# Load order, dummy matmuls, one PSUM drain and the weight folds in the first stage of a fused linear-attention and MLP kernel

## The chip, the cores and the metric

The kernel runs on one core of one Trainium2 chip. The metric is the device time of one execution in microseconds. Every execution also lists its span (first to last instruction) and the mean clock that TensorE was granted; the time is about 2.1 us more than the span (183.99 and 181.9). The engines are PE (TensorE matmul), PEld (TensorE weight load), DVE (VectorE), ACT (ScalarE), POOL (GpSimd) and SP (SyncE, which here only issues DMAs). PSUM is the name of the memory of the banks that the matmuls here write (`bank<-wv,xnT` in the profile) and that ScalarE or DVE then reads out (`xnT<-bank`, 0.60 us for 128x512; "drains").

## The reference, cut to what matters

With `x` of 2048 tokens by 448, two branches read the same normalised input:

```python
xn  = layernorm(x)                                  # (2048, 448)
# branch A: linear attention, 16 heads of 28
q, k, v = split(xn @ wqkv)
phi(t)  = concat(softmax(t @ w_phi), softmax(-(t @ w_phi)))    # per head
o   = phi(q) @ (phi(k).T @ v) / (phi(q) @ sum(phi(k)) + 1e-6)
A   = o @ wo
# branch B: token-shift mixer and MLP
h   = gelu(layernorm(xn) @ w1)
x1  = xn + shifted(h) @ w2
B   = x1 + gelu(layernorm(x1) @ w3) @ w4
out = x + A + B
```

The kernel multiplies `w_phi` into the K and Q columns of `wqkv` on the chip ("folds": `wpk`, `wpq`), so that K and Q need one matmul each. Tokens are worked in 16 tiles of 128.

## The kernel before: the parts that the change touches

Every operation is recorded and later emitted on its engine in program order. Semaphore waits are derived from what each operation reads and writes. All matmuls are recorded by one helper line, L203, transposes by L207, ScalarE's activations by L211, other elementwise work by L215, and DMA transposes by L218; so the profile's lines are told apart by their operands.

The loads. SP and ACT issue to a DMA queue each (on the page of before q1 with 12.64 MB and q10 with 1.92 MB, which is what ACT's issues add up to; cuts marked `...`):

```python
        load_x(0, 1)                 # SP
        load_x(1, 1, "ACT")
        load_x(2, 1)                 # SP
        load_x(3, 1, "ACT")
        load_lap(wv, A_wqkv[:, 896:1344], ("ACT", "SP"))   # two halves of wv
        load_x(4, 2)
        load_x(6, 2)
        load_wT(1); load_wT(0)       # 8 DMA transposes of K's and Q's weights, on SP
        ...
        load_lap(w1, B_w1, ("ACT", "ACT"))
        load_x(8, 4, "ACT")
        load_x(12, 4, "ACT")
        R.dma(wphi[0:CR, :, :], ..., "ACT")
```

The normalisation of the 16 tiles is a sequence on DVE and POOL. The statistics of tile `i` stand on DVE ahead of the scaling of tile `i-1`:

```python
        for i in range(10):
            ln1_stats(i, 1, 0)                 # DVE: bn_stats, bn_aggr; POOL: rs
            if i not in (0, 4):
                ln1_apply(dve, i - 1)          # DVE: xn of tile i-1
            if i == 3:
                ln1_apply(dve, 3)
        ...
        for i in range(12, NT):
            xn_Td(i)                           # DMA transposes of tiles 12 to 15, on SP
```

The first matmul stage. There are four pairs of PSUM banks, 0 to 3. `xn_T(i, b)` transposes tile `i` on TensorE into pair `b`, and ScalarE copies it to `xnT`. `V(i, k)` is half `k` of the V projection of tiles `i, i+1`; `v_out(i, b)` drains it (ScalarE). `W(g, m, k)` is half `k` of W1's column pair `m` for token group `g`; `w1_out` is its gelu (ScalarE). `FO(1, ..)` folds K's weights, `FO(0, ..)` Q's; their second half is followed by DVE's casts to `wpk` or `wpq`. `spin` issues dummy matmuls that nothing reads.

```python
        vps = {i: v_pair(i, b) for i, b in ((0, 2), (2, 3), (4, 2), (6, 3), (8, 3), (10, 2))}
        wps = {(g, m): w1_pair(g, m, b) for g, m, b in (..., (3, 0, 0), (3, 2, 2))}
        fps = {(t, m): fold_pair(t, m, b) for t, m, b in ((1, 0, 2), (1, 2, 3), (0, 0, 1), (0, 2, 3))}

        spin(19, 256)
        play([(xn_T, 0, 0), (spin, 3, 256), (xn_T, 1, 1), (spin, 2, 256), V(0, 0), (xn_T, 2, 0), V(0, 1), (xn_T, 3, 1),
              ...
              (w1_out, 0, 2, 1), V(4, 0), V(6, 0), V(4, 1), (v_out, 4, 2), V(6, 1), W(1, 0, 0), (xn_T, 8, 2),
              (v_out, 6, 3), W(1, 2, 0), (xn_T, 9, 2), W(1, 0, 1), (xn_T, 10, 2), W(1, 2, 1), (xn_T, 11, 2),
              (w1_out, 1, 0, 0), (w1_out, 1, 2, 1), V(8, 0), V(10, 0), V(8, 1), (v_out, 8, 3), V(10, 1),
              ...
              FO(1, 2, 0), W(2, 2, 1), (w1_out, 2, 2, 1), FO(1, 2, 1), W(3, 0, 0), W(3, 2, 0), FO(0, 0, 0),
              W(3, 0, 1), (w1_out, 3, 0, 0), FO(0, 0, 1), FO(0, 2, 0), W(3, 2, 1), (w1_out, 3, 2, 2), FO(0, 2, 1)])
```

The loop that follows starts with K's pair (banks of pair 1), then W2's pair (pair 2), and goes on with Q.

The softmax here doesn't subtract the row's maximum and nothing guards it: scores larger than these inputs give would overflow.

## Time and profile before

| | before |
|---|---|
| timed executions | 182.07, 182.23, 182.28 us |
| the profiled execution | 183.99 us, span 181.9, clock 0.991 |
| TensorE busy | 174.4 us, 96% of the span |
| granted clock 0.50 | from 7.93 to 11.35 us |

Part 2 of the page of before cuts the span into 40 slices. Each digit is the busy share of TensorE, or the granted clock, in tenths:

```profile
PE   7699999999999999999999999999999999999993
PEclk9879999999999999999999999999999999999999
```

The clock dips in the second and third slices, 4.5 to 13.6 us, and nowhere else in this row. The table by windows of before, cut at the clock's own steps, shows what came ahead of the dip. The columns are the window, its length, then busy time of PE, PEld, DVE, ACT and POOL with the count of instructions, then the granted clock, the DMA share and GB/s:

```profile
4.52:7.93 3.41, 1.91 (x27) 0.97 (x25) 2.73 (x9) 0.93 (x2) 2.55 (x7) 1.00 1.02 330
7.93:11.35 3.42, 3.42 (x31) 2.14 (x32) 2.62 (x7) 0.76 (x2) 1.66 (x5) 0.50 1.43 336
11.35:14.76 3.41, 3.33 (x39) 2.31 (x39) 3.31 (x10) 2.13 (x4) 2.46 (x7) 1.00 0.91 126
```

In a window of 3.41 us TensorE was busy for 1.91 us, and the next 3.41 us ran at half clock. These are lines of the timeline of before; each has its start, its length, the operation with its shapes, and in brackets the idle time ahead of it with what ended that:

```profile
7.91 1.91 PE L203 MATMUL bank<-wv,xnT 64*128 64x448 bf16 x8 [0.77 <-DMA wv<-in_A_wqkv_dram]
...
23.22 0.29 PE L207 MATMUL bank<-ident,xn 64*128 64x64 bf16 x8 [0.34 <-POOL wpq L215]
...
24.40 2.93 PE L203 MATMUL bank<-wv,xnT 64*128 64x448 bf16 x28
27.18 1.89 PE L203 MATMUL bank<-xnT,w 64*112 64x512 bf16 x16
...
31.00 1.93 PE L203 MATMUL bank<-xnT,w 64*112 64x512 bf16 x16
...
35.28 0.93 PE L203 MATMUL bank<-wpk,xnT 64*128 64x448 bf16 x7 [0.23 <-DVE wpq L215]
35.86 1.10 PE L203 MATMUL bank<-w,hT 64*128 64x448 bf16 x8
```

In order: the first V pair waits for `wv`; the transposes of tile 10 wait; the V pair of tile 8 starts at 24.40; W1's second last group (tiles 8 to 11) at 27.18, its last (tiles 12 to 15) at 31.00; K's first pair waits for the casts of `wpq`; W2's first pair starts at 35.86 with no wait of its own.

### The profile page before, as it was taken

What the parts mean: (1) busy time and instruction counts of PE and PEld (TensorE: products, weight loads), DVE (VectorE), ACT (ScalarE), POOL (GpSimd) and SP (SyncE); (2) the same over time, 40 slices, a digit from 0 to 9 for tenths busy, and PEclk for the clock granted to TensorE, in tenths of its full rate; (3) what the DMA queues carried; (4) which work ended last, traced back from release to release, by engine and by line L of the source; (5) the groups of instructions that cost most, each with busy time, mean ns of one, the idle gap of its engine ahead of it and who ended that gap; (6) DMA issues with size and microseconds to landing.
All of it is one profiled execution on the core that took longest, in us unless ns stands there. A gap on an engine that the chain in (4) does not pass through costs nothing.

```text
span 181.9 us, 5076 instructions
## 1 busy us (share of the span) xinstructions
PE 174.4 (96%) x2196; PEld 100.3 (55%) x2196; DVE 112.5 (62%) x282; ACT 82.5 (45%) x92; POOL 96.0 (53%) x140
## 2 busy tenths in 40 slices
PE   7699999999999999999999999999999999999993
PEld 5357546645587976566445454554555545545451
DVE  5799816669799699835465984641545517465521
ACT  2247875579778887744822422422224213224000
POOL 4666850007779989990065939562350622622740
PEclk9879999999999999999999999999999999999999
DMA  5993277990001110113011341323323120311331
GB/s 125 343 227 71 51 91 212 395 364 15 0 4 29 32 29 4 41 34 73 4 29 32 60 89 30 83 66 71 64 55 83 38 74 0 83 29 29 83 85 45
DMA packets 32981, 14.87 MB, mean 82 GB/s; under 512 B 24704, under 2 KB 32448, under 8 KB 32960
## 3 DMA queue, kind: packets, MB, share of 16 engines
q1 hardware_dynamic: 30192, 12.64, 28.7%
q10 hardware_dynamic: 2768, 1.92, 3.3%
q8 instruction: 17, 0.28, 0.7%
q14 instruction: 4, 0.03, 0.1%
HBM read 7.08 MB, written 1.84 MB: 49 GB/s over the span
## 4 chain that ended last, share of the span: by engine, by line
PE 74%; DVE 10%; POOL 6%; DMA 5%; issue 1%; SPq 1%; ACT 1%; DVEq 0%
PE bank L203 74%; DMA xtok<-in_A_x_dram 4%; DVE xn L215 3%; DVE st L215 3%; POOL rs L215 2%; POOL phik L215 2%; DVE ksum L215 2%; DMA gT<-g_tok 1%; DVE mv L215 1%; POOL xn L215 1%; DVE wpq L215 1%; SPq L221 1%; POOL mv L215 1%; DVE rks L215 1%; ACT phik L211 1%
## 5 line engine op out<-in xcount | busy, mean ns | idle before, releaser
L211 ACT ACTIVATE phik<-bank 128x1024 bf16<-128x1024 f32 (+1 forms) x44 | 42.4, 986 | 62.1 <-PE bank L203 62.1
L203 PE MATMUL bank<-gT,w 64*128 64x512 bf16 x392 | 50.5, 377 | 0.6 <-DMA gT<-g_tok 0.3
L215 DVE TENSOR_TENSOR vaug<-bank,vaug 128x464 f32<-128x464 f32 (+3 forms) x65 | 32.6, 512 | 23.9 <-PE bank L203 22.3
L203 PE MATMUL bank<-w,phik 64*128 64x448 bf16 (+1 forms) x420 | 45.0, 349 | 0.1
L215 POOL TENSOR_TENSOR xnT<-vaug 128x196 bf16<-128x196 f32 (+1 forms) x32 | 18.1, 588 | 47.6 <-DVE vaug L215 47.6
L203 PEld LDWEIGHTS bank<-w,phik 64*128 64x128 bf16 (+1 forms) x420 | 21.7, 94 | 21.7 <-PE bank L203 0.5
L215 POOL TENSOR_TENSOR phik<-phik,rks 128x896 bf16<-128x896 bf16 x16 | 26.8, 1699 | 10.5 <-DVE rks L215 10.5
L203 PEld LDWEIGHTS bank<-gT,w 64*128 64x128 bf16 x392 | 18.4, 94 | 18.4 <-ACT phik L211 1.6
L215 POOL TENSOR_TENSOR vaug<-xn,xtok 128x448 f32<-128x448 bf16 x16 | 16.2, 1034 | 1.2 <-DVE vaug L215 1.2
L215 DVE TENSOR_REDUCE ksum<-phik 128x32 f32<-128x896 bf16 x16 | 16.8, 1048 | 0.0
L203 PE MATMUL bank<-w,hT 64*128 64x448 bf16 (+1 forms) x128 | 16.4, 349 | 0.2 <-DVE xn L215 0.2
L203 PE MATMUL bank<-wv,xnT 64*128 64x448 bf16 x112 | 15.2, 378 | 1.1 <-DMA wv<-in_A_wqkv_dram 0.8
L215 DVE TENSOR_TENSOR xn<-bank,xn 128x256 bf16<-128x256 f32 (+1 forms) x32 | 10.2, 381 | 9.7 <-PE bank L203 9.7
L203 PE MATMUL bank<-xnT,wpq 64*128 64x512 bf16 x112 | 16.1, 376 | 0.0
L203 PE MATMUL bank<-wpk,xnT 64*128 64x448 bf16 x112 | 15.4, 349 | 0.2 <-DVE wpq L215 0.2
L215 DVE RECIPROCAL vaug<-bank 128x16 f32<-128x16 f32 x16 | 4.1, 257 | 17.9 <-PE bank L203 17.9
L203 PE MATMUL bank<-xnT,w 64*112 64x512 bf16 x112 | 15.0, 381 | 0.0
L203 PE MATMUL bank<-wo,xnT 64*128 64x448 bf16 (+1 forms) x106 | 13.4, 349 | 0.0
L215 POOL TENSOR_TENSOR rs<-mv,mhalf 128x1 f32<-128x1 f32 (+2 forms) x17 | 11.7, 690 | 1.4
L215 POOL TENSOR_SCALAR g_tok<-xn,rs 128x512 bf16<-128x512 bf16 x16 | 12.2, 773 | 0.2
L211 ACT ACTIVATE xnT<-bank 128x512 bf16<-128x512 bf16 x12 | 7.1, 597 | 9.6 <-PE bank L207 9.6
L203 PEld LDWEIGHTS bank<-w,hT 48*128 48x128 bf16 (+1 forms) x128 | 8.6, 94 | 4.8 <-DVE xn L215 1.2
(63 smaller groups left out, 181.2 us busy)
## 6 DMA issues: line engine op xcount, KB each, us to landing
w<-in_B_w_dram SPq DMA_DIRECT2D x2, 896.0 KB, 6.6
out_dram<-vaug SPq DMA_DIRECT2D x15, 112.0 KB, 1.9
w<-in_B_w_dram SPq DMA_DIRECT2D x1, 1568.0 KB, 11.9
xtok<-in_A_x_dram ACTq DMA_DIRECT2D x2, 448.0 KB, 8.4
xtok<-in_A_x_dram SPq DMA_DIRECT2D x2, 224.0 KB, 7.0
w<-in_B_w_dram ACTq DMA_DIRECT2D x2, 224.0 KB, 7.1
wo<-in_A_wo_dram SPq DMA_DIRECT2D x2, 224.0 KB, 8.3
w<-in_B_w_dram SPq DMA_DIRECT2D x1, 392.0 KB, 3.7
```

The costliest lines, as they stand in the source:

```text
L203: self.op("PE", lambda e: e.matmul(out, lhsT, rhs, start=start, stop=stop, skip_group_check=True), [out], [lhsT, rhs], tile=self._tile(lhsT))
L211: self.op("ACT", lambda e: e.activation(out, in_, func, **kw), [out], [in_] + aps)
L215: self.op(eng, lambda e: getattr(e, name)(out, *args, **kw), [out], aps)
L221: self.op(eng, lambda e: e.dma_start(out, in_), [out], [in_], dma=True)
```

## The change

It has three parts, which I call A, B and C from here on. A: the first half of `wv` is loaded ahead of `x3`, and four dummy matmuls instead of two bridge the time to the first V pair; the aim is that V starts sooner (the wait for `wv` was 0.77 us) and that the clock does not fall to 0.50. B: the V drain of tile 6 moves behind the transposes of tiles 9 and 10, which should not wait for ScalarE (0.34 us). C: the Q folds are done sooner, so that K's first pair does not wait for DVE's casts (0.23 us).

```diff
-        load_x(3, 1, "ACT")
-        load_lap(wv, A_wqkv[:, 896:1344], ("ACT", "SP"))
+        load_lap(wv, A_wqkv[:, 896:1344], ("ACT", "SP"))
+        load_x(3, 1, "ACT")
...
-        play([..., (xn_T, 1, 1), (spin, 2, 256), V(0, 0), ...
+        play([..., (xn_T, 1, 1), (spin, 4, 256), V(0, 0), ...
...
-              (v_out, 6, 3), W(1, 2, 0), (xn_T, 9, 2), W(1, 0, 1), (xn_T, 10, 2), W(1, 2, 1), (xn_T, 11, 2),
+              W(1, 2, 0), (xn_T, 9, 2), W(1, 0, 1), (xn_T, 10, 2), (v_out, 6, 3), W(1, 2, 1), (xn_T, 11, 2),
...
-              ..., W(3, 0, 0), W(3, 2, 0), FO(0, 0, 0),
-              W(3, 0, 1), (w1_out, 3, 0, 0), FO(0, 0, 1), FO(0, 2, 0), W(3, 2, 1), (w1_out, 3, 2, 2), FO(0, 2, 1)])
+              ..., W(3, 0, 0), FO(0, 0, 0), W(3, 2, 0),
+              FO(0, 0, 1), FO(0, 2, 0), W(3, 0, 1), (w1_out, 3, 0, 0), W(3, 2, 1), (w1_out, 3, 2, 2), FO(0, 2, 1)])
```

More of the change, by code (lines that the diff above doesn't have):

```diff
@@ L752, in bass_parallel_sum__linear_kernel_hedgehog__mixer_s_mlp__prompt_kernel @@
         spin(19, 256)
-        play([(xn_T, 0, 0), (spin, 3, 256), (xn_T, 1, 1), (spin, 2, 256), V(0, 0), (xn_T, 2, 0), V(0, 1), (xn_T, 3, 1),
+        play([(xn_T, 0, 0), (spin, 3, 256), (xn_T, 1, 1), (spin, 4, 256), V(0, 0), (xn_T, 2, 0), V(0, 1), (xn_T, 3, 1),
               (spin, 2, 256), V(2, 0), (v_out, 0, 2), W(0, 0, 0), (xn_T, 4, 2), V(2, 1), (v_out, 2, 3),
@@ L756, in bass_parallel_sum__linear_kernel_hedgehog__mixer_s_mlp__prompt_kernel @@
               (w1_out, 0, 2, 1), V(4, 0), V(6, 0), V(4, 1), (v_out, 4, 2), V(6, 1), W(1, 0, 0), (xn_T, 8, 2),
-              (v_out, 6, 3), W(1, 2, 0), (xn_T, 9, 2), W(1, 0, 1), (xn_T, 10, 2), W(1, 2, 1), (xn_T, 11, 2),
+              W(1, 2, 0), (xn_T, 9, 2), W(1, 0, 1), (xn_T, 10, 2), (v_out, 6, 3), W(1, 2, 1), (xn_T, 11, 2),
               (w1_out, 1, 0, 0), (w1_out, 1, 2, 1), V(8, 0), V(10, 0), V(8, 1), (v_out, 8, 3), V(10, 1),
               (v_out, 10, 2, "DVE"), W(2, 0, 0), W(2, 2, 0), FO(1, 0, 0), W(2, 0, 1), (w1_out, 2, 0, 0), FO(1, 0, 1),
-              FO(1, 2, 0), W(2, 2, 1), (w1_out, 2, 2, 1), FO(1, 2, 1), W(3, 0, 0), W(3, 2, 0), FO(0, 0, 0),
-              W(3, 0, 1), (w1_out, 3, 0, 0), FO(0, 0, 1), FO(0, 2, 0), W(3, 2, 1), (w1_out, 3, 2, 2), FO(0, 2, 1)])
+              FO(1, 2, 0), W(2, 2, 1), (w1_out, 2, 2, 1), FO(1, 2, 1), W(3, 0, 0), FO(0, 0, 0), W(3, 2, 0),
+              FO(0, 0, 1), FO(0, 2, 0), W(3, 0, 1), (w1_out, 3, 0, 0), W(3, 2, 1), (w1_out, 3, 2, 2), FO(0, 2, 1)])
         def w2_norm(i):
```

## The prediction

> **What bounds it now.** TensorE is busy 96% of the 181.9 us span (page, part 1), and 74% of the chain that ended last is matmuls (part 4). From 35.3 us on it waits only about 1 us in all (list of waits), so only the first 35 us can give anything, and a saving there should reach the end.
>
> Four losses lie there (timeline of TensorE, table by windows):
> - The granted clock is 0.50 from 7.93 to 11.35 us, one stretch of 3.41 us. [...] In the window before it, 4.52 to 7.93, TensorE was busy only 1.9 us. The first V pair then takes 1.91 us for 8 matmuls, later ones about 0.8. Up to 1.7 us is lost.
> - 0.77 us idle until wv lands (7.58 and 7.78 us; first matmul 7.91).
> - 0.34 us idle at 23.2 us before the transposes of tile 10. The waits name POOL; I believe it is ScalarE's copy of tile 9 (to 23.07), which ran behind tile 6's V drain (21.67 to 22.58).
> - 0.23 us idle at 35.28, K's first pair waiting for VectorE's wpq casts (from 33.94).
>
> Normalised tiles are not the limit: tile 10 is ready at 19.6 and transposed at 23.2; the room is about 2 us.
>
> **The change, costed.**
> 1. wv's first half ahead of x3: lands perhaps 2 us sooner, x3 that much later (its statistics start at 6.39, so nearly free). But ScalarE issues DMAs until 6.96 and copies tile 1 only from 7.50 to 8.09, which the pair's second matmul needs. So the pair starts 0.25 us sooner and gains about 0.1.
> 2. Two more dummies: about 0.2 us more activity, inside idle time. With the pair's sooner start, the window rises from 1.9 to about 2.4 us busy of 3.41. Whether that keeps the clock this trace doesn't show; I give it 55%. If kept: V0 ends near 9.0 and tile 4's transposes come at 12.4 instead of 13.5; about 1.2 us gained.
> 3. V drain of tile 6 moved: tile 10's transposes about 0.2 sooner, but the drain now ends near 24.75, and the V pair of tile 8, which writes the same banks, must wait for it: 24.8 instead of 24.4. Net loss about 0.3.
> 4. Q folds sooner: K's wait (up to 0.5) goes. But gelu of the last W1 group is later: its second drain ends near 36.05 instead of 35.78, and the W2 pair needs those banks. Net between 0.3 gained and 0.3 lost.
>
> **Sum.** Clock kept: about 181.3. Clock lost: about 182.5. I say 181.8 us, range 180.8 to 182.9. Faster by over 2%: 0.02; within 2%: 0.97; slower: 0.01.
>
> **What would show it.** Step 1: wv landing before 7 us, first V matmul near 7.65, the second still near 8.1. Step 2: no 0.50 clock between 7.9 and 11.4, 8 V matmuls in about 0.9 us. Step 3: no idle at tile 10, a new wait of TensorE for ScalarE's V drain before tile 8's V pair. Step 4: no wait for wpq, a wait for ScalarE's gelu before the first W2 pair.
>
> **What would make it wrong.** [...] a late x3 holding up VectorE's statistics by more than the 2 us of room.

Two passages on what sets the clock are cut out of it, and marked: a sentence on the stretch of half clock, and two clauses of the last paragraph, the second of which said that the times might split by about 1.2 us. The trace did not show what they said of the clock. No term of the sum is cut: 55% of 181.3 and 45% of 182.5 make the 181.8 us.

## The result, and the profile after

The changed kernel took 182.89, 183.22, 182.91 and 182.61 us (median 182.9); before took 182.07 to 182.28 in four executions (median 182.19). The ratio is 1.004, 95% interval 1.0022 to 1.0058. Ratios in this document are the mean time of one kernel's runs over that of the other's runs of the same rounds, so they are not quite the ratios of the medians that are quoted. All four executions of the changed kernel show a clock of 0.998 to 1.00, and the profiled one has a span of 180.8 us: 1.1 us less than the profiled one of before, although the timed executions are 0.7 us slower. The two profiles are thus not of the same kind.

The first two windows of the table of the changed kernel, cut at the same times as before (its own first clock step is at 5.23 us, and 5.23 to 8.64 us has TensorE busy for 2.89):

```profile
4.52:7.93 3.41, 2.89 (x33) 1.51 (x33) 2.87 (x9) 1.19 (x2) 2.32 (x6) 1.00 1.01 327
7.93:11.35 3.42, 3.34 (x44) 1.88 (x42) 2.42 (x8) 2.00 (x3) 1.80 (x6) 1.00 1.20 301
```

TensorE's lines in the timeline of the changed kernel that answer to those of before:

```profile
7.43 1.15 PE L203 MATMUL bank<-wv,xnT 64*128 64x448 bf16 x8
...
21.09 0.29 PE L207 MATMUL bank<-ident,xn 64*128 64x64 bf16 x8
...
22.88 2.82 PE L203 MATMUL bank<-wv,xnT 64*128 64x448 bf16 x28 [0.43 <-ACT vaug L211]
25.54 1.89 PE L203 MATMUL bank<-xnT,w 64*112 64x512 bf16 x16
...
29.78 1.07 PE L203 MATMUL bank<-xnT,w 64*112 64x512 bf16 x8 [0.42 <-ACT hT L211]
...
33.45 0.92 PE L203 MATMUL bank<-wpk,xnT 64*128 64x448 bf16 x7
34.85 0.93 PE L203 MATMUL bank<-w,hT 64*128 64x448 bf16 x8 [0.48 <-ACT hT L211]
```

Each wait that the change aimed at is gone: `wv`, tile 10, the casts. Three others have come: 0.43 us for the moved V drain (`vaug`) ahead of tile 8's V pair, 0.42 us ahead of W1's last group, and 0.48 us for the gelu ahead of W2's first pair. One line of DVE's timeline of the changed kernel is new as well, the statistics of `x3`:

```profile
6.80 0.63 DVE L215 BATCH_NORM_STATS2 st<-xtok 128x6 f32<-128x448 bf16 x1 [0.19 <-DMA xtok<-in_A_x_dram]
```

To say where 0.7 us came from, I first needed an ordinary execution of before to compare with.

### The profile page after: what moved, and what is told of

Same layout as the page of the kernel before. It is cut to its first block, busy times and chain, and to the rows that moved or that the text cites. A ratio compares the mean times of both kernels' runs of the same rounds, so it can differ in the third digit from the quotient of the medians.

```text
span 180.8 us, 5080 instructions
## 1 busy us (share of the span) xinstructions
PE 173.3 (96%) x2198; PEld 100.1 (55%) x2198; DVE 112.6 (62%) x282; ACT 82.7 (46%) x92; POOL 95.7 (53%) x140
## 4 chain that ended last, share of the span: by engine, by line
PE 74%; DVE 10%; POOL 6%; DMA 4%; ACT 2%; issue 2%; ACTq 0%; DVEq 0%
PE bank L203 74%; DVE xn L215 3%; DVE st L215 3%; DMA xtok<-in_A_x_dram 3%; POOL rs L215 2%; POOL phik L215 2%; DVE ksum L215 2%; DMA gT<-g_tok 1%; DVE mv L215 1%; ACT hT L211 1%; POOL mv L215 1%; DVE rks L215 1%; ACT phik L211 1%; ACTq L221 0%; ACT vaug L211 0%
## 5 line engine op out<-in xcount | busy, mean ns | idle before, releaser
L203 PE MATMUL bank<-wpk,xnT 64*128 64x448 bf16 x112 | 14.7, 349 | 0.0
L203 PE MATMUL bank<-wv,xnT 64*128 64x448 bf16 x112 | 13.6, 351 | 0.7 <-ACT vaug L211 0.4
L203 PEld LDWEIGHTS bank<-w,hT 64*128 64x128 bf16 (+1 forms) x128 | 8.4, 94 | 5.7 <-DVE xn L215 1.2
```

Of the source, the lines that this page charges most:

```text
L203: self.op("PE", lambda e: e.matmul(out, lhsT, rhs, start=start, stop=stop, skip_group_check=True), [out], [lhsT, rhs], tile=self._tile(lhsT))
```

## The experiments

Sixteen kernels ran, four to a chip, each beside 11 executions of before on the same chip. All gave correct results. Means are over the executions at full clock (0.998 to 1.00), and the difference is to the mean of the executions of before beside them.

| run | edit on before | executions us | clock 0.991 | mean | difference |
|---|---|---|---|---|---|
| e0_before_again | none | 181.91 to 182.00 | 0 of 5 | 181.95 | -0.23 |
| a_only | A | 181.99 to 182.54 | 0 of 5 | 182.26 | +0.07 |
| b_only | B | 182.29 to 184.00 | 1 of 6 | 182.44 | +0.26 |
| c_only | C | 182.04 to 183.87 | 2 of 6 | 182.25 | +0.06 |
| after_again | A, B, C | 182.40 to 183.62 | 0 of 6 | 182.89 | +0.65 |
| a_and_c | A, C | 182.05 to 182.81 | 0 of 6 | 182.30 | +0.06 |
| t10_other_bank | tile 10 in other banks | 181.66 to 182.15 | 0 of 5 | 181.89 | -0.35 |
| c_banks_swapped | C, W1's last banks exchanged | 181.65 to 181.80 | 0 of 5 | 181.73 | -0.51 |
| x3_later | x3 behind half of w1 | 182.87 to 183.42 | 0 of 4 | 183.17 | +0.93 |
| few_dummies | five dummies out | 181.83 to 184.52 | 3 of 6 | 182.75 (with the 184.52) | +0.52 |
| few_dummies_wv_early | five dummies out, wv early | 182.38 to 183.40 | 3 of 6 | 182.75 | +0.52 |
| t10_and_c_swapped | both mends | 180.90 to 181.71 | 0 of 6 | 181.21 | -1.03 |
| a_and_b | A, B | 182.43 to 183.00 | 0 of 5 | 182.57 | +0.42 |
| b_and_c | B, C | 182.05 to 182.43 | 0 of 5 | 182.27 | +0.13 |
| after_third | A, B, C | 182.34 to 182.78 | 0 of 5 | 182.50 | +0.35 |
| mended_and_dummies | both mends, two more dummies | 181.28 to 181.97 | 0 of 6 | 181.66 | -0.49 |

The first row is the yardstick: the same code came out 0.23 us below before (ratio 0.9986, interval 0.9974 to 0.9998). A difference of 0.2 us or less in one row says little by itself; there I rely on where the waits stand in the profiles.

### What is an ordinary execution of before? (e0_before_again)

No edit.

> The kernel before, unchanged, to see what its ordinary execution looks like. Theory 1 (the profile of before that I predicted from was an odd execution: it took 183.99 us where the timed ones took 182.07 to 182.28, and the difference of 1.8 us is the one stretch at clock 0.50): most of these runs have clock 1.00, spans of 180.0 to 180.3 us and times of 182.1 to 182.3; at most one or two in five show clock 0.991, and those are near 184.0. Rival (the clock drop is ordinary and the profile only costs time elsewhere): clock 0.991 in all of them, with spans near 181.9.

Measured: five executions, all at clock 0.999 or 1.00, spans 179.8 and 179.9. None of the 44 executions of before that ran beside the experiments shows 0.991 either. Theory 1 holds (times and spans 0.1 to 0.2 us under its range): the profile that I predicted from was an uncommon execution. The windows of the ordinary one, cut as before's (its own first clock step is at 5.54 us, and 5.54 to 8.95 us has 2.90 busy):

```profile
4.52:7.93 3.41, 2.85 (x31) 1.28 (x31) 2.90 (x9) 1.20 (x2) 2.50 (x7) 1.00 0.98 319
7.93:11.35 3.42, 3.34 (x44) 1.90 (x42) 2.57 (x7) 2.00 (x3) 1.88 (x5) 1.00 1.14 354
```

And TensorE's lines in the timeline of this ordinary execution, in the same order as those shown of before:

```profile
7.24 1.36 PE L203 MATMUL bank<-wv,xnT 64*128 64x448 bf16 x8
...
21.35 0.29 PE L207 MATMUL bank<-ident,xn 64*128 64x64 bf16 x8 [0.34 <-ACT xnT L211]
...
22.53 2.93 PE L203 MATMUL bank<-wv,xnT 64*128 64x448 bf16 x28
25.30 1.89 PE L203 MATMUL bank<-xnT,w 64*112 64x512 bf16 x16
...
29.13 1.94 PE L203 MATMUL bank<-xnT,w 64*112 64x512 bf16 x16
...
33.41 0.93 PE L203 MATMUL bank<-wpk,xnT 64*128 64x448 bf16 x7 [0.24 <-DVE wpq L215]
33.99 1.10 PE L203 MATMUL bank<-w,hT 64*128 64x448 bf16 x8
```

The first V pair starts at 7.24 without any wait for `wv`, sooner than in the changed kernel (7.43). So in an ordinary execution part A has nothing to win at the start. Set against these lines, the profile of the changed kernel gives a full account. W1's second last group starts at 25.30 here and at 25.54 there (+0.24, part B). W1's last group starts at 29.13 and 29.78 (+0.65, of which 0.41 are new, the wait of 0.42 us). W2's first pair starts at 33.99 and 34.85 (+0.86, of which 0.21 are new, part C). The spans are 179.9 and 180.8. Nothing else is lost: the 0.9 us are all there by 35 us.

The wait at tile 10 is here put down to ScalarE's copy, not to POOL, which settles that question of the prediction.

### Part A alone

```diff
-        load_x(3, 1, "ACT")
-        load_lap(wv, ...)
+        load_lap(wv, ...)
+        load_x(3, 1, "ACT")
...
-(spin, 2, 256), V(0, 0)
+(spin, 4, 256), V(0, 0)
```

> Before with the load order and the two more dummies alone (parts A). Theory 1: with the clock kept in both kernels, A gives only what the earlier first V pair is worth, at most 0.4 us before tile 12 is needed, and perhaps nothing at the end because the transposes by DMA of tiles 12 to 15 then hold TensorE: time 181.8 to 182.3. Rival (A is what costs: x3 later delays the statistics): 182.5 to 182.9.

Measured: 182.3 us, ratio 1.0003 (0.9991 to 1.0015). A gives nothing. In its profile the first V pair starts at 7.42, and W1's last group at 29.08 against 29.13. The landing records of the trace show the exchange: `wv`'s first half lands at 4.40 instead of 7.02, and `x3` at 6.43 instead of 4.16. Both are on ScalarE's queue: the one put ahead came 2.62 us sooner, the one put behind 2.27 us later.

### Part B alone

```diff
-(v_out, 6, 3), W(1, 2, 0), (xn_T, 9, 2), W(1, 0, 1), (xn_T, 10, 2), W(1, 2, 1), ...
+W(1, 2, 0), (xn_T, 9, 2), W(1, 0, 1), (xn_T, 10, 2), (v_out, 6, 3), W(1, 2, 1), ...
```

> Before with the V drain of tile 6 behind two transposes alone (part B). Theory: the V pair of tile 8 waits about 0.4 us for that drain, as the profile after shows, while the wait at tile 10 that it removes was 0.2 to 0.3: 182.3 to 182.6 us. Rival (the drain costs nothing, because what follows waits anyway for the transposes by DMA): 182.1 to 182.3.

Measured: 182.47 us, ratio 1.0028 (1.0002 to 1.0053); without the one execution at clock 0.991 (184.00) the mean is 0.26 us over before. TensorE's timeline of this run:

```profile
22.88 2.82 PE L203 MATMUL bank<-wv,xnT 64*128 64x448 bf16 x28 [0.43 <-ACT vaug L211]
25.54 1.89 PE L203 MATMUL bank<-xnT,w 64*112 64x512 bf16 x16
```

The V pair of tile 8 writes the banks that the moved drain still reads: 22.88 instead of 22.53, and 25.54 instead of 25.30 for what follows. The theory holds, with the 0.3 us of the prediction; but 0.26 us is hardly more than equal code differed by (0.23), so the place of the wait says more than the time.

### Part C alone

```diff
-W(3, 0, 0), W(3, 2, 0), FO(0, 0, 0), W(3, 0, 1), (w1_out, 3, 0, 0), FO(0, 0, 1), FO(0, 2, 0), W(3, 2, 1), ...
+W(3, 0, 0), FO(0, 0, 0), W(3, 2, 0), FO(0, 0, 1), FO(0, 2, 0), W(3, 0, 1), (w1_out, 3, 0, 0), W(3, 2, 1), ...
```

> Before with the Q folds sooner alone (part C). Theory: the wait of K's first pair for VectorE's casts goes (0.2 to 0.5 us gained), but the first W2 pair waits about 0.5 us for ScalarE's gelu: 182.1 to 182.6 us. Rival: the folds cost nothing or gain: 181.7 to 182.1.

Measured: 182.42 us, ratio 1.0019 (0.9992 to 1.0045); two of six executions are at clock 0.991, and the other four are 0.06 us over before. Its profile is one of the slow-clock ones, so I compare distances in it, which the clock's dip at 8 to 11 us no longer touches:

```profile
36.09 0.93 PE L203 MATMUL bank<-w,hT 64*128 64x448 bf16 x8 [0.48 <-ACT hT L211]
```

W1's last group starts at 30.93 in this profile, so W2's first pair comes 5.16 us after it, against 4.86 us (33.99 less 29.13) in the ordinary execution of before. The wait for the casts is gone, but a longer one for the gelu stands in its place. In the time of the whole kernel, C alone is not told from nothing.

### The whole change again, and without B

after_again is the changed kernel; a_and_c undoes B in it.

> The changed kernel unchanged, on the chip of its neighbours here. Theory (the loss is the sum of part B, a wait for the V drain, about 0.3, and part C, a wait for gelu, about 0.2, and both are in every execution): 182.6 to 183.0 us, clock 1.00 in every run, and the first matmul of W1's last group waiting again for something near 29.6 us. Rival (the wait at 29.4 to 29.8 us in the profile after, where the DMA transpose of tile 15 landed at 29.58 instead of 28.9, was a chance of that execution): that wait is gone in this profile and the time is nearer 182.5.

> The changed kernel with part B undone (the V drain of tile 6 back in its place). Theory: TensorE no longer waits 0.43 us for the drain before tile 8's V pair, waits 0.34 us before tile 10 again, and the time falls by 0.2 to 0.3 against the changed kernel run here: 182.3 to 182.6. Rival (the parts do not add; the transposes by DMA of tiles 12 to 15 hold TensorE anyway): the same as the changed kernel within 0.1.

Measured on the same chip: 182.72 us with B (ratio 1.0032, 1.0014 to 1.005) and 182.11 without (1.0003, 0.9989 to 1.0017). B's removal is worth more here (0.6 us) than B alone costs (0.26). The time fell by twice what the theory of a_and_c had (0.2 to 0.3). The wait ahead of W1's last group came again in after_again, so the rival that it was one chance execution falls. This line is from DVE's timeline of after_again:

```profile
7.51 0.63 DVE L215 BATCH_NORM_STATS2 st<-xtok 128x6 f32<-128x448 bf16 x1 [0.94 <-DMA xtok<-in_A_x_dram]
```

And these are from TensorE's:

```profile
9.84 0.29 PE L207 MATMUL bank<-ident,xn 64*128 64x64 bf16 x8 [0.27 <-DVE xn L215]
...
30.26 1.07 PE L203 MATMUL bank<-xnT,w 64*112 64x512 bf16 x8 [0.27 <-ACT hT L211]
```

Here `x3` landed at 7.48, DVE stood still 0.94 us for it, the transposes of tiles 2 and 3 came late (9.84 for tile 3 instead of 9.25 in the ordinary execution), and everything after them. The wait at 30.26 is put down to ScalarE's gelu, but the gelu that frees those banks ended near 29.9 (the first of two that start at 28.91 and take 1.99 us together), and the DMA transpose of tile 15 landed at 30.06. The first matmul comes 0.14 to 0.20 us after that landing here, in the changed kernel (29.58 and 29.78) and in t10_other_bank below (28.74 and 28.88), where the profile does name the DMA.

### Is a late x3 a cost at all? (x3_later)

```diff
-        load_x(3, 1, "ACT")          # ahead of wv
...
-        load_lap(w1, B_w1, ("ACT", "ACT"))
+        R.dma(w1[:, 0:2, :], ..., "ACT")
+        load_x(3, 1, "ACT")
+        R.dma(w1[:, 2:4, :], ..., "ACT")
```

> The suspected cost of part A made large: the kernel before, with x3 issued behind the first halves of wv and of w1 on ScalarE's queue instead of ahead of wv. Theory (the statistics, the casts and the DMA transposes of the 16 tiles are one rigid chain from x3 to W1's last group, with only 0.1 to 0.2 us of room at its end): x3 lands near 8.5 to 9 us instead of 4.1, its statistics start 2 to 2.5 us later than the 6.55 of the ordinary run, the DMA transpose of tile 15 lands that much later than 28.98, and the time rises by nearly as much, to 183.9 to 184.6 us. Rival (the prediction's: about 2 us of room before the tiles are needed): 182.2 to 182.8.

Measured: 183.19 us, ratio 1.0047 (1.0031 to 1.0062). Both theories missed: the cost is clear, but 0.93 us instead of nearly 2. `x3` landed at 8.32. DVE's timeline of this run:

```profile
8.35 0.63 DVE L215 BATCH_NORM_STATS2 st<-xtok 128x6 f32<-128x448 bf16 x1 [1.73 <-DMA xtok<-in_A_x_dram]
```

And TensorE's:

```profile
9.54 0.29 PE L207 MATMUL bank<-ident,xn 64*128 64x64 bf16 x8 [0.82 <-DVE xn L215]
```

DVE lost 1.73 us, and tile 2, whose scaling stands behind the statistics of `x3` on DVE, reached TensorE at 9.54 instead of 8.26. So a late `x3` costs first through tile 2 at the start. The end of the sequence followed by less: the transpose of tile 15 landed at 30.32, 1.33 us later than in the ordinary execution (28.98), and TensorE came to W1's last group late anyway (30.57). What the theory called one rigid chain does stretch, by some 0.4 us.

### What does the clock answer to? (few_dummies, few_dummies_wv_early)

```diff
-(xn_T, 0, 0), (spin, 3, 256), (xn_T, 1, 1), (spin, 2, 256), V(0, 0)
+(xn_T, 0, 0), (xn_T, 1, 1), V(0, 0)
```

> The kernel before without the five dummy matmuls between the first transposes and the first V pair, to see what the clock answers to. Theory [...]: half or more of the runs show clock 0.991 or less, and each of those is 1.5 to 2.0 us over the others, near 184. Rival (the clock drop is set by the chip, not by TensorE's idling): 0 or 1 of 6 runs show it, as in the kernel before.

> The same without those dummies, with wv's first half ahead of x3. Theory [...]: clearly fewer halved clocks than in the run without dummies beside it, at most 2 of 6. Rival (the earlier wv does nothing for the clock, because ScalarE's copies of tiles 0 and 1 hold the pair anyway): as many as there.

Measured: 3 of 6 executions at clock 0.991 without the dummies, against 0 of 11 of before on the same chip (183.51 to 183.58 against 181.83 and 181.90), and 3 of 6 also with `wv` early (183.16 to 183.40 against 182.38 and 182.56). One more of each was slow (184.52 and 183.32) at a listed clock of 1.00; neither was traced, and why is open. So the rival of the first run missed: with the dummies out, and TensorE idle for longer, the halved clock came in 6 of 12 executions, with them in 0 of 11. The early `wv` alone did not prevent it: the theory of the second run missed, as many halved as beside it. The profile of few_dummies, cut at its own steps:

```profile
4.37:7.78 3.41, 1.54 (x23) 0.73 (x22) 3.06 (x9) 1.09 (x2) 2.54 (x7) 1.00 0.94 290
7.78:11.19 3.41, 3.41 (x32) 1.75 (x31) 2.42 (x7) 0.72 (x2) 1.79 (x6) 0.50 1.12 363
```

I cut the first 14 us of all 18 profiles into windows of 3.41 us, the distance of the clock's steps in before (4.52, 7.93 and 11.35), laid so that a step of each profile's own clock is a border. Three windows were followed by half clock, with TensorE, transposes included, busy for 1.54 (few_dummies), 1.91 (before) and 1.93 us (c_only). Every other window at full clock, from the first recorded step on, was followed by full clock, and had 2.32 us (x3_later) or more. That is what these profiles hold; how the clock is set beyond that is not shown. The windows of c_only, x3_later and a_only, the last of which is needed below:

```profile
4.47:7.89 3.42, 1.93 (x26) 0.95 (x24) 2.89 (x9) 1.19 (x2) 2.51 (x7) 1.00 0.94 302
...
7.28:10.69 3.41, 2.32 (x26) 0.75 (x26) 1.59 (x5) 1.06 (x2) 0.82 (x3) 1.00 1.11 352
...
4.51:7.93 3.42, 2.56 (x33) 1.42 (x33) 2.87 (x9) 1.19 (x2) 2.54 (x7) 1.00 1.01 326
```

The place of the steps in the kernel differs from profile to profile: the first recorded one lies at 4.37 to 4.52 us in the three halved profiles, and in all others but one at 4.03 or between 5.2 and 7.3 us. The one is a_only: there the step lay at 4.51, nearly where it lay in before (4.52), and TensorE was then busy 2.56 us instead of 1.91, and the clock stayed up. In this one execution part A did what it was meant to do.

The executions that need it are few. Among executions with the original loads and dummies, 3 of 82 in the experiments show 0.991 (0 of 49 of before itself, 3 of 33 of its variants), and the first profile of before is a fourth. With part A it was none of 31. At that rate A saves under 0.1 us on average (3 of 82 times the 1.5 us between the means of the halved and the full executions of c_only, an estimate), and the two counts don't prove a difference.

### Can B's aim be had without its wait? (t10_other_bank)

```diff
-(xn_T, 10, 2)
+(xn_T, 10, 3)
```

> A mend of the aim of part B: the kernel before, with the transposes of tile 10 written to the other pair of banks, which the V drain of tile 6 has already left. Theory: TensorE's 0.34 us wait at tile 10 goes and the V pair of tile 8 starts about 0.4 us sooner (near 22.1 instead of 22.5), but W1's last group then waits for the DMA transpose of tile 15 (landing near 28.9), so only 0.1 to 0.2 us reaches the end: 181.9 to 182.1 us. Rival (nothing else holds it): 181.7.

Measured: 181.81 us, ratio 0.9981 (0.9969 to 0.9993). TensorE's timeline:

```profile
20.87 0.29 PE L207 MATMUL bank<-ident,xn 64*128 64x64 bf16 x8
...
21.85 2.85 PE L203 MATMUL bank<-wv,xnT 64*128 64x448 bf16 x28
...
28.88 1.94 PE L203 MATMUL bank<-xnT,w 64*112 64x512 bf16 x16 [0.52 <-DMA xnT<-xn]
```

No wait at tile 10, the V pair of tile 8 at 21.85 instead of 22.53, and then a wait of 0.52 us for the DMA transpose. Of 0.68 us gained, 0.25 reach W1's last group (28.88 against 29.13), and even these match a landing of tile 15 that came 0.24 us sooner here (28.74 against 28.98), to which the profile shows no link from the edit. The mechanism is that of the theory; the time lies 0.1 us under its range, and 0.35 us in the mean is only 0.12 more than equal code differed by. It also measures the room that the prediction put at 2 us: in an ordinary execution tile 15 lands at 28.98 and its use starts at 29.13, 0.15 us later. As the use came 0.14 to 0.25 us after the landing also in the profiles where TensorE waited for it, next to no room is left.

### Can C's aim be had without its wait? (c_banks_swapped)

C, with the banks of W1's last two pairs exchanged:

```diff
-(3, 0, 0), (3, 2, 2)          # in wps: W(3, 0) in pair 0, W(3, 2) in pair 2
+(3, 0, 2), (3, 2, 0)
```

> A mend of part C: the folds sooner, as in the change, but the two W1 pairs of the last group exchange their banks, so that the W2 pair takes the banks of the gelu that ends first. Theory: neither the 0.24 us wait for the casts nor the 0.48 us wait for gelu is left, so K's and W2's first pairs come 0.3 to 0.5 us sooner: 181.6 to 181.9 us. Rival (C costs by something else, such as the later start of the exponentials): 182.1 to 182.4.

Measured: 181.74 us, ratio 0.9972 (0.996 to 0.9984), and the least scatter of all edits. TensorE's timeline:

```profile
29.44 1.07 PE L203 MATMUL bank<-xnT,w 64*112 64x512 bf16 x8 [0.23 <-DVE wpk L215]
...
33.84 0.97 PE L203 MATMUL bank<-w,hT 48*128 48x448 bf16 x8
```

W2's pair now takes the banks of the gelu that ends first. It starts 4.40 us after W1's last group instead of 4.86 (before) or 5.16 (C alone), with no wait. That shows what C lacked. The exchange has its own small price, 0.23 us for K's casts ahead of W1's last group.

### The two mends together

> The two mends together on the kernel before: tile 10 in the other banks, and the folds sooner with the banks of W1's last two pairs exchanged. Theory: they act at different places, but the exchange makes W1's last group wait 0.23 us for the casts of K's folds, and those come sooner now, so the gains add except for what the DMA transpose of tile 15 takes: 0.3 plus 0.4 us, 181.4 to 181.6 us. Rival (the transpose of tile 15 takes all of the first gain): 181.7 to 181.8.

Measured: 181.16 us, ratio 0.9944 (0.9929 to 0.9958), better than both kernels: 1.03 us under before in the mean, more than the 0.35 and 0.51 of the two mends, and under the 181.4 to 181.6 us of the theory. TensorE's timeline:

```profile
28.90 1.07 PE L203 MATMUL bank<-xnT,w 64*112 64x512 bf16 x8 [0.47 <-DMA xnT<-xn]
...
33.27 0.97 PE L203 MATMUL bank<-w,hT 48*128 48x448 bf16 x8
```

The wait for K's casts is hidden under the wait for tile 15, which is there anyway. That explains why the gains do not merely share; the rest of the excess is within the 0.23 us by which equal code can differ.

### Do the parts add? (a_and_b, b_and_c, after_third, mended_and_dummies)

> Load order, dummies and the moved V drain, without the folds. Theory 1 (parts A and B interact: A delays the normalised tiles in those executions where x3 lands after about 6.6 us, B delays TensorE, ScalarE's drains and what follows): 182.6 to 182.9 us, scatter of 0.5 us or more. Theory 2 (they add): 182.4 to 182.5.

> The moved V drain and the sooner folds, without load order and dummies. Theory 1 (B and C add, 0.25 plus 0.1): 182.4 to 182.6 us in the runs at full clock, scatter under 0.4 us, with perhaps one run in six at clock 0.991 near 184. Theory 2 (B and C interact): 182.8 to 183.0.

> The changed kernel once more, on the same chip as the pairs of parts. Both theories: 182.7 to 183.0 us. If the pairs are near 182.5 and this is near 182.9, all three are needed for the loss; if a_and_b is near it, A with B makes it.

> The two mends (181.16 us in its run) with four dummies instead of two before the first V pair. The dummies lie in idle time unless wv lands before about 7 us, then they push the first V pair back by up to 0.2 us: 181.1 to 181.5 us, full clock in all runs. If it is over 181.5, the dummies cost more than they can save.

Measured on one chip: A and B 182.45 us (ratio 1.0023, 1.0011 to 1.0035), B and C 182.4 (1.0007, 0.9995 to 1.0019), the whole change 182.42 (1.0019, 1.0008 to 1.0031). On this chip the whole change is 0.35 us over before; A, B and C alone sum to 0.39 (0.07, 0.26 and 0.06). So the parts add, here, within the 0.23 us by which equal code differed (A and B together were 0.42, B and C 0.13). The expectation of after_third, 182.7 to 183.0 us by both theories, missed. In the first result and in after_again the whole change was 0.65 to 0.7 us over. The difference is not settled. What the profiles show is that the wait ahead of W1's last group (0.42, 0.27, 0.40 us) stands in all three profiles of the whole change, where `x3` landed at 6.77, 7.48 and 6.87 us, and in none of the profiles of a_only, a_and_c and a_and_b, where it landed at 6.43, 6.03 and 6.45. few_dummies_wv_early, with A's load order and without B and C, had `x3` at 7.14 us and a wait of 0.36 us there, put down to the DMA. B and C cannot move `x3`, as nothing of them is issued by then. Nor is `x3` the only difference: SP's instruction that issues the second of the four DMA transposes took 2.55, 2.31 and 2.53 us in the first three and 1.99, 2.29 and 2.08 in the others. I have not shown what part of this is chance.

Two more dummies on the mended kernel gave 181.69 us, over the limit of 181.5 that I had set. They ran on another chip than the mended kernel without them, and the profile's wait ahead of W1's last group is 0.94 us, to 29.04, where that of the other ends at 28.90. The profile names DVE's cast for the 0.94 us, but the cast that frees these banks ended at 28.27; tile 15 landed at 28.84 here and at 28.65 there, so that the DMA transposes set both, as far as the profiles tell. No gain from the dummies is seen in six executions.

## Why the prediction was wrong, point by point

**The step that failed is the base.** The prediction set out from "The granted clock is 0.50 from 7.93 to 11.35 us", and credited the change with 55% of "about 1.2 us gained" for keeping the clock. The timed executions of before had kept it. The profiled execution took 183.99 us, the timed ones 182.07 to 182.28; the difference of 1.8 us is about half of one 3.41 us stretch at clock 0.50 (1.7 us, an estimate). All of this was in the data before I predicted. 182.2 us is the time at full clock, so the sum "Clock kept: about 181.3" subtracted a loss that was not in 182.2, and the "Clock lost" branch, 182.5, is what the remaining terms give from the right base. The measured 182.9 us lies 0.4 above that, and here a second step failed, "the room is about 2 us": in the profile of the changed kernel W1's last group waits 0.42 us for tile 15, which lands 0.60 us later than in the ordinary execution (29.58 against 28.98). Of these, 0.14 stand ahead of SP's first issue of the four transposes (21.92 against 21.78) and 0.46 in the longer issue of the second (2.55 against 2.09), which nothing here ties to the change.

- **wv, the first V pair and step 1.** "So the pair starts 0.25 us sooner and gains about 0.1." In the ordinary execution it starts at 7.24, and at 7.42 to 7.43 with part A. The prediction read ScalarE's last DMA issue (to 6.96) and the copies (7.50 to 8.09) from the uncommon profile; in e0_before_again the issues end at 6.19 and the second copy runs from 7.03 to 7.63. `wv` landed before 7 us as said, but nothing waited for it any more.
- **x3 "nearly free" and "the room is about 2 us".** Wrong, and for the same reason: in the slow-clock profile TensorE arrives about 1.9 us late at W1's last group (31.00 against 29.13), which looked like room for the tiles. The prediction took the room from tile 10 and did not ask when the DMA transposes land: tile 15's lands at 29.11 in that profile. In ordinary executions the room is 0.15 us at most, and DVE waited for x3 in all three profiles of the whole change (0.19, 0.94 and 0.30 us). Made large, it costs 0.93 us.
- **The clock.** The direction was right: the two dummies with the sooner `wv` do lift TensorE's busy time, from 1.91 us in before (4.52 to 7.93) to 2.56 us in a_only (4.51 to 7.93; predicted 2.4), and the clock after it was 1.00 instead of 0.50. That fits the windows of the other profiles, but one profile does not prove it. Its weight was wrong: 4 executions in some 80 of before and its variants, not all of them.
- **Part B.** Right in direction, place and size: 24.8 against 24.4 was predicted for tile 8's V pair, measured 22.88 against 22.53, with the wait for the drain that it named; 0.26 us in the time, predicted 0.3.
- **Part C.** Right in mechanism: the wait for the casts goes (0.24 us), a wait for the gelu comes (0.48 us). "Net between 0.3 gained and 0.3 lost" held, at a loss of 0.2 to 0.3 us at W2's first pair, of which the time of the whole kernel shows hardly any.
- **Releaser of tile 10's wait.** ScalarE, as guessed; the profiles of e0_before_again, a_only, c_only and others name it (before and few_dummies name POOL).

What stays open is why the whole change lost 0.35 us on one chip and 0.65 to 0.7 on others, and what lengthens one of SP's four issues.

## What to carry to other kernels

Compare the time of the profiled execution with the timed ones first; if they differ by as much as one effect in the trace is worth, that effect is not in the time that you are to change. Moving a drain or a fold did not remove its wait here, as the next user of the same banks now came close behind it: a different bank removed both waits here (0.34 us at tile 10, 0.48 us at W2's first pair), where a different order only exchanged them (0.34 for 0.43 us, 0.24 for 0.48 us). When a stage is sped up, look at once for the next input that was just in time, here the DMA transposes with 0.15 us to spare at most.

## What else the traces show of the clock and of SP's issues

- In the three windows that were followed by half clock (TensorE busy for 1.54, 1.91 and 1.93 of 3.41 us), no single gap was over 0.81 us (c_only; 0.77 in before, 0.76 in few_dummies): the idle time was spread over each window.
- The clock's fall cost 1.5 us (c_only, between means) to 1.8 us (before) of 182, about 1%, in 4 of some 80 executions with the original loads and dummies. That is more than the whole change was worth, and it fell into the one profiled execution.
- Ahead of its first record the clock is printed as 1.00, but the dummy matmuls stand further apart there. In before the first record is at 4.52 us; those that start ahead of it stand 0.21 us apart, those after it 0.11. In the changed kernel it is at 5.23 us, with 0.21 ahead of it and 0.11 to 0.12 after it. So I take the first record for the step from half to full clock.
- SP's instruction that issues a DMA transpose of tiles 12 to 15 took 1.22 to 1.27 us for three of the four in the profiles of before and of the changed kernel, and 2.18 and 2.55 us for the fourth (the third in before, the second in the changed kernel). A 16 KB instruction fetch began 0.25 and 0.05 us ahead of that one; that it is the cause is not shown.
